# Key scales of the first three pairs and the fold of two halved blocks: one operand moved from SBUF to PSUM

## The chip, the core and the metric

The kernel runs on one core of a Trainium2 chip. A core has five engines that work in parallel, each in program order: TensorE (PE) multiplies matrices into PSUM, VectorE (DVE), ScalarE (ACT) and GpSimd (POOL) work on tiles in SBUF and, DVE and ACT, in PSUM, and SyncE (SP) issues transfers. The engines wait for each other through semaphores. The metric is the device time of one execution in microseconds (us); the time of a version is the median of its runs.

## What is computed

An attention block with a state that is updated token by token (B = 4, H = 8, S = 768, D = 48), and behind it a gated feed-forward layer over 3072 tokens:

```python
k_n = k / (np.linalg.norm(k, axis=-1, keepdims=True) + 1e-06)
state = zeros((B, H, D, D))
for t in range(S):
    y[:, :, t] = einsum('bhd,bhde->bhe', q[:, :, t], state)
    v_old = einsum('bhde,bhd->bhe', state, k_n[:, :, t])
    state += beta[:, :, t] * outer(k_n[:, :, t], v[:, :, t] - v_old)
x = y.transpose(0, 2, 1, 3).reshape(3072, 384)
h = x @ w_in                  # 384 x 2048
out = (h * np.cos(h)) @ w_out # 2048 x 384
```

## The kernel before

**Units and pairs.** The sequence is cut into 24 units of 32 tokens (C = 32). Unit n belongs to pair m = n // 2. Within a unit, the token-by-token recurrence becomes a triangular system: the Gram matrix of the unit's keys (`gram`, line 641, products at L652) goes to PSUM, its strictly triangular part, scaled by the keys' step sizes, is inverted, and the inverse, applied to the values minus what the state gives, yields the state's update. The state passes from unit to unit, so the units form a chain. Beside it the feed-forward layer is spread out over PE, ACT, DVE and POOL as soon as a unit's output rows are there, and the weights are rounded on their way in (`narrow_split` on ACT, L525 and L529; `narrow_shift` on DVE, L533; `narrow_add` on POOL, L537: one per 512 or 384 columns).

**Three kinds of inversion.** Units 0 and 1 are inverted by repeated doubling on PE, with DVE between the steps (`doubling`, lines 681 to 758: L691, L701, L706, products at L736, then L744, L749, L752, L756 on DVE). From unit 4 on, a pair's scaled Gram blocks are written to DRAM (`gram_put`, line 799, DMA issued at L810), read back in another layout (`gram_get`, L823), inverted column by column on POOL (`invert`, L856 and L863, two instructions a column), and returned through DRAM. Pair 1 (`HALVED = 1`, units 2 and 3) goes the same way with halved blocks: each 32 x 32 block is cut into two diagonal blocks of 16 x 16 (HC = 16), put in one tile by `fold` (line 767), and one block between them, which PE applies later from `off_blocks`. Part of pair 1's columns is inverted on DVE.

**Scales.** For the pair's keys, ACT squares (L554), DVE sums (L559), POOL takes the root with a power (`norms_root`, L571) and `scale` on DVE (lines 578 to 595) makes from the norm: `knrm` = norm + 1e-6 (L582), `krec` = 1 / knrm^2 (L584 and L585), `bs` = beta * krec (L587) and `bz`, which is `bs` for one half of the partitions and zero for the other, by a mask `odd` of two columns (L590). Units 0 to 3 have a scale each, of 8 columns; from unit 4 on there is one for a pair, of 16 columns. `weigh` (lines 597 to 612, product at L607) multiplies a pair's values by `knrm`; `gram_keys` (line 660; L664 for units 0 and 1, L673 for the others) multiplies the Gram blocks by `bs` or `bz` on their way from PSUM to SBUF, and `gram_queries` (line 779; L784 or L792) takes the other half of the same bank with a mask.

**The fold before** works on one SBUF tile `g`: it scales its first 16 columns by a mask of the partitions, in place (L770), adds the last 16 columns scaled by the other mask (L771), and writes the last 16 columns by the first mask to `off_blocks` (L775):

```python
f = gs[n] = g[:, :, 0:HC]
nc.vector.tensor_scalar(f, f, in_half[:, 0:1], None, op0=ALU.mult)
nc.vector.scalar_tensor_tensor(
    out=f, in0=g[:, :, HC:], scalar=in_half[:, 1:2], in1=f,
    op0=ALU.mult, op1=ALU.add,
)
nc.vector.tensor_scalar(
    off_blocks[n][:, :, HC:], g[:, :, HC:], in_half[:, 0:1], None, op0=ALU.mult
)
```

**Fillers.** While PE has nothing else to do in the opening, `keep_warm` (lines 490 to 495, product at L492) multiplies a constant tile into `p_out[:, 0]`. `p_out` (line 485) is one PSUM bank of [128, 2, 256] floats; later it takes the feed-forward layer's output products (L1274, L1332). Its columns `[:, 1, 192:]` are used by nothing.

**What sets the order.** The kernel is written as tasks, each with an engine, a cost, what it depends on, and what PSUM bank or SBUF tile it makes or frees (`add(..., deps, makes=..., uses=...)`, from line 1471 on for a unit). Class `Order` (lines 60 to 237) holds the sequence of the tasks as a stored list; `uses` names the buffers whose last use a task is, and a task that makes a buffer can't stand ahead of them. When the tasks are written out, each instruction is pinned behind the one ahead of it on its engine (lines 1862 to 1894), so every engine's order is the stored one, and semaphores for data and buffers come on top. The bank with the tag "two" (one buffer) holds in turn a unit's turned keys and queries (`turn`, L619), its Gram products, and the later products of the state. Transfers that go through SP stand in one queue, and they share eight hardware semaphores in turn, so that a transfer waits for the eighth ahead of it.

Of the kernel before, what the change touches and what calls it, by code (L numbers as in the profile page):

```python
# [13 lines left out]
ALU = mybir.AluOpType  # L14
# [45 lines left out]
class Order:  # L60
# [147 lines left out]
    def add(  # L208
        self, key, engine, cost, emit, deps=(), makes=(), uses=(), moves=0.0, due=1e9,
        other=None,  # L210
    ):
        assert key not in self.tasks, key
        self.tasks[key] = emit, set(deps), makes, uses
        for t in uses:
            self.users[t] = self.users.get(t, 0) + 1
        for tag, t in makes:
            self.tiles[t] = tag
# [22 lines left out]
def kernel(  # L240
# [32 lines left out]
    nc = tc.nc  # L273

    B, H, S, D = q.shape
# [49 lines left out]
    def half(i):  # L325
        return slice(DP * i, DP * i + DP)
# [13 lines left out]
    def by_parity(t):  # L340
        return t.rearrange("p (j a) i -> p a j i", a=2)
# [5 lines left out]
    DOUBLED, HALVED, HC = 2, 1, C // 2  # L347
    eye16 = early[:, EYE : EYE + HC * HC]
    in_flat = in_sum.rearrange("p a b c -> p (a b c)")
    half_zt, off_blocks = (  # L350
        {
            2 + i: t[:, at + i * H * C : at + (i + 1) * H * C].rearrange("p (h c) -> p h c", c=C)
            for i in range(2)
        }
        for t, at in ((early, HALF_ZT), (in_flat, OFFS))
    )
# [75 lines left out]
    odd = consts[:, 128 + C : 130 + C]  # L432
    in_half = consts[:, 130 + C : 132 + C]
# [8 lines left out]
    for b in range(B):  # L442
        nc.gpsimd.dma_start(
            out=bq[C * b : C * b + H].rearrange("p n t -> p (n t)"), in_=beta[b]
# [19 lines left out]
    bt = const.tile([128, NU, H], FP, name="bt")  # L464
# [18 lines left out]

    HM = DM // 2
    p_out = psum.tile([128, 2, 256], FP, name="p_out", tag="o", bufs=1)


    out_begun = []
# [46 lines left out]
    def narrow_add(t):  # L535
# [4 lines left out]
    sums, squares, scales, kq_ts, p_ts, p_gs, gs, grams, gbs, z_drs, zs, zts = (  # L540
        {} for _ in range(12)
    )
# [35 lines left out]
    def scale(m, part):  # L578

        n = part.stop - part.start  # L580
        bs, bz, knrm = (t[:, part] for t in scales[m])
        nc.vector.tensor_tensor(out=knrm, in0=knrm, in1=tiny[:, 0:n], op=ALU.add)  # L582
        krec = work.tile([128, 2, H], FP, name="krec")[:, 0:n]
        nc.vector.tensor_tensor(out=krec, in0=knrm, in1=knrm, op=ALU.mult)  # L584
        nc.vector.reciprocal(krec, krec)  # L585
        first = 2 * m + part.start
        nc.vector.tensor_tensor(  # L587
            out=bs, in0=bt[:, first : first + n], in1=krec, op=ALU.mult
        )
        nc.vector.tensor_tensor(  # L590
            out=bz,
            in0=bs[:, :, :, None].to_broadcast([128, n, H, 2]),
            in1=odd[:, None, None, :].to_broadcast([128, n, H, 2]),
            op=ALU.mult,
        )

    def weigh(m):

        vp, knrm = vps[m], scales[m][2]
        if 2 * m >= PLAIN_TURNS:  # L600

            t = work.tile([128, 2, H], FP, name="krec")
            nc.vector.tensor_copy(t[:, :, 0::2], knrm[:, :, 0::2])
            for i in range(2):
                nc.vector.tensor_copy(t[half(i), :, 1::2], knrm[half(1 - i), :, 1::2])
            knrm = t
        nc.vector.tensor_tensor(  # L607
            out=vp,
            in0=vp,
            in1=knrm[:, :, :, None].to_broadcast([128, 2, H, D]),  # L610
            op=ALU.mult,
        )

    def turn(n, tag):
# [45 lines left out]
    def gram_keys(n):  # L660
        if n < DOUBLED:
            bz = scales[n // 2][1][:, n % 2]
            for par in range(2):
                nc.vector.tensor_tensor(  # L664
                    out=power(n)[:, OFF, par].rearrange("p j (o i) -> p j o i", i=C),
                    in0=p_gs[n][:, par, :, 0, None].to_broadcast([128, NP, 2, C]),
                    in1=bz[:, par::2, :, None].to_broadcast([128, NP, 2, C]),
                    op=ALU.mult,
                )
            return  # L670
        g = gs[n] = work.tile([128, H, C], FP, name="g")
        bs = scales[n // 2][0][:, n % 2]
        nc.vector.tensor_tensor(  # L673
            out=by_parity(g),
            in0=p_gs[n][:, :, :, 0],
            in1=bs.rearrange("p (j a) -> p a j", a=2)[:, :, :, None].to_broadcast(wide),
            op=ALU.mult,
        )


    def power(n):
        whole = (in_sum, w_sum)[n].rearrange("p a b c -> p (a b c)")
        return whole[:, 0 : POWERS * H * C].rearrange(
            "p (x a j i) -> p x a j i", a=2, j=NP, i=2 * C
        )
# [79 lines left out]
        nc.gpsimd.memset(in_flat[:, OFFS : OFFS + 2 * H * C], 0.0)  # L765

    def fold(n):
        g = gs[n]
        f = gs[n] = g[:, :, 0:HC]
        nc.vector.tensor_scalar(f, f, in_half[:, 0:1], None, op0=ALU.mult)  # L770
        nc.vector.scalar_tensor_tensor(  # L771
            out=f, in0=g[:, :, HC:], scalar=in_half[:, 1:2], in1=f,
            op0=ALU.mult, op1=ALU.add,
        )
        nc.vector.tensor_scalar(  # L775
            off_blocks[n][:, :, HC:], g[:, :, HC:], in_half[:, 0:1], None, op0=ALU.mult
        )

    def gram_queries(n):
        if n < DOUBLED:  # L780
# [180 lines left out]
    first, spare = {}, {}  # L961
# [127 lines left out]
    def gate_tile(p, s, unit):  # L1089
        return g_tiles[order.place["gates", p, s, unit]]  # L1090
# [302 lines left out]
    def store(p, i, cols=slice(0, DM)):  # L1393
# [7 lines left out]
        for b in range(B):  # L1401
# [9 lines left out]
            x=2, x_sum=XS, turns=2, g=GATES, o=2, o_out=2,  # L1411
# [3 lines left out]
    add = order.add  # L1415
# [26 lines left out]
    def doubling(n):  # L1442
        add(("double_first", n), "DVE", 0.75, lambda: double_first(n), [("gram_keys", n)])
        add(("double_rest", n), "DVE", 0.7, lambda: double_rest(n), [("double_first", n)],
            uses=[("g_gram", n)])
        last = [[("double_first", n)], [("double_first", n)]]
        for level in range(len(LEVELS)):
            for par in range(2):
                deps = last[par] + ([("double_rest", n)] if level == 1 else [])
                key, tile_of = ("double", n, level, par), ("p_d", n, level, par)  # L1450
                add(key, "PE", 0.6, lambda level=level, par=par: double(n, level, par), deps,
                    makes=[("h", tile_of)])
                last[par] = []
                for what, emit, levels in (
                    ("copy", double_copy, COPIES), ("turn", double_turn, TURNS),
                    ("add", double_add, ADDS),
                ):
                    if level not in levels:
                        continue
                    then = ("double_" + what, n, level, par)  # L1460
                    add(then, "ACT" if what == "copy" else "DVE", 0.35,
                        lambda emit=emit, level=level, par=par: emit(n, level, par),
                        [key], uses=[tile_of])
                    last[par].append(then)
                if level == 3:
                    add(("double_turn", n, 3, par), "DVE", 0.3,
                        lambda par=par: double_turn(n, 3, par), last[par])
                    last[par] = [("double_turn", n, 3, par)]
        return last[0] + last[1]

    def unit(n):
        m, second = n // 2, n % 2
# [17 lines left out]
        part = slice(second, second + 1) if n < 4 else slice(0, 2)  # L1490
# [18 lines left out]
        if n < PLAIN_TURNS:  # L1509
# [6 lines left out]
                uses=[("p_t", n)])  # L1516
        else:
# [11 lines left out]
            uses=[("kq_t", n)])  # L1529
        add(("gram_keys", n), "DVE", 0.46, lambda: gram_keys(n),  # L1530
            [("gram", n), scaled],
            uses=[("p_g", n), ("scales", m)])
        add(("gram_queries", n), "DVE", 0.46, lambda: gram_queries(n), [("gram_keys", n)],
            uses=[("p_g", n)])
        if n < DOUBLED:
            inverted = doubling(n)
        else:
            inverted = [("get", n)]
            if m == HALVED:
                add(("fold", n), "DVE", 0.62, lambda: fold(n), [("gram_keys", n), ("half_tiles",)])  # L1540
            add(("gram_put", n), "SP", 0.45 if n < PLAIN_TURNS else 1.8, lambda: gram_put(n),
                [("fold" if m == HALVED else "gram_keys", n)], makes=[] if second else [("g_dr", ("g_dr", m))],
                uses=[("g_gram", n)], moves=0.85)
            if second:
                inverse(m)
            add(("get", n), "SP", 1.9, lambda: get(n),
                [("put", m)] + ([("clear", i) for i in range(ZTS)] if m != HALVED else []),
                makes=[("zt", ("zt", n))] if m != HALVED else [], uses=[("z_dr", m)], moves=0.9)
# [6 lines left out]
            uses=[("vp", m)] if n else [])  # L1555
        few = 0.7 if n < PLAIN_TURNS else 0.61
        ready = [("right", n)] + inverted
        if m == HALVED:
# [7 lines left out]
                uses=[("p_v", n)])  # L1566
# [3 lines left out]
            uses=[("rhs", n) if n else ("vp", m)] + ([] if n < DOUBLED else  # L1570
                  [("u_half", n)] if m == HALVED else [("zt", n)]))
# [354 lines left out]
```

## Time and profile before

| | us |
|---|---|
| median of 3 runs | 641.02 |
| the three runs | 639.75, 641.02, 642.40 |
| the profiled execution's own time | 643.07 |
| its span in the profile | 641.3 |
| mean granted TensorE clock | 0.989 of full speed |

The profiled execution is a run of its own, above the three timed ones; 1.77 us of it lie outside the span. The profile records when each instruction of each engine began and ended. Its parts used here: the busy time of each engine; the chain of work that ended last, followed back from the end, with for each step its start, its duration, the engine and what it writes and reads; the timeline, which lists instructions in order of time (start, duration of the stretch, engine, line, operation, names and shapes, and in square brackets the idle time ahead of it with what ended it; a row that ends in "x6" is a group of six records of one kind); and the table of windows, which gives for a stretch its length and then, for each engine in turn, the busy time and the number of instructions, in the order PE, PEld (weight loads), DVE, ACT, POOL, and then the granted TensorE clock, the busy share of the DMA engines and their GB/s.

Of the lines that the change touches, the trace has in the first 65 us: L582 five times, with a mean of 0.156 us; L584 0.169, L585 0.213, L587 0.168 and L590 0.187, also five times; L607 0.95 to 1.04 in the four products that read `knrm` itself; L770, L771 and L775 twice each. L607 reads `knrm` through a copy from pair 4 on (0.96 to 1.02). The filler L492 stands 70 times in the records, all between 1.3 and 80.1 us.

### The profile page before, as it was taken

What the parts mean: (1) busy time and instruction counts of PE and PEld (TensorE: products, weight loads), DVE (VectorE), ACT (ScalarE), POOL (GpSimd) and SP (SyncE); (2) the same over time, 40 slices, a digit from 0 to 9 for tenths busy, and PEclk for the clock granted to TensorE, in tenths of its full rate; (3) what the DMA queues carried; (4) which work ended last, traced back from release to release, by engine and by line L of the source; (5) the groups of instructions that cost most, each with busy time, mean ns of one, the idle gap of its engine ahead of it and who ended that gap; (6) DMA issues with size and microseconds to landing.
All of it is one profiled execution on the core that took longest, in us unless ns stands there. A gap on an engine that the chain in (4) does not pass through costs nothing.

```text
span 641.3 us, 24183 instructions
## 1 busy us (share of the span) xinstructions
PE 622.4 (97%) x10174; PEld 578.0 (90%) x10174; DVE 495.7 (77%) x1030; ACT 297.2 (46%) x528; POOL 435.2 (68%) x775
## 2 busy tenths in 40 slices
PE   7997989999999999999999999999999999999997
PEld 5776877987799999999999999999999999999997
DVE  5896556679989998898787898888888776666682
ACT  3655556554234453543543634743643553545440
POOL 4274688588788788887898887886883883112231
PEclk7999899999999999999999999999999999999999
DMA  9886646854435541655416345243304102000001
GB/s 190 215 180 165 145 100 139 169 102 65 95 58 77 94 67 34 113 87 99 76 23 105 51 72 100 52 62 66 74 2 82 41 2 42 18 2 26 2 25 26
DMA packets 209382, 50.37 MB, mean 79 GB/s; under 512 B 200921, under 2 KB 204281, under 8 KB 209273
## 3 DMA queue, kind: packets, MB, share of 16 engines
q1 hardware_dynamic: 159224, 35.62, 29.3%
q10 hardware_dynamic: 49744, 12.66, 9.8%
q8 instruction: 80, 1.31, 0.9%
q0 software_dynamic: 304, 0.54, 0.4%
q14 instruction: 30, 0.24, 0.1%
HBM read 38.55 MB, written 10.22 MB: 76 GB/s over the span
## 4 chain that ended last, share of the span: by engine, by line
PE 77%; DMA 6%; POOL 6%; DVE 5%; issue 2%; SPq 1%; ACT 1%; ACTq 0%; DVEq 0%; POOLq 0%
PE p_out L1332 26%; PE p_h L1250 25%; PE p_h L1076 6%; PE p_kq L907 3%; PE p_s L1004 3%; PE p_out L1274 3%; POOL part L856 2%; POOL z L863 2%; PE p_u L979 2%; PE p_kq L1034 2%; DMA kp<-in_k_dram 2%; PE p_g L652 2%; DMA gb<-g_dr 2%; PE p_h L1332 2%; DMA g_dr<-g 1%
## 5 line engine op out<-in xcount | busy, mean ns | idle before, releaser
L856 POOL TENSOR_TENSOR part<-z,gb 128x126 f32<-128x126 f32 (+24 forms) x317 | 140.2, 442 | 44.6 <-DMA gb<-g_dr 12.4
L863 POOL TENSOR_TENSOR z<-z,part 128x126 f32<-128x126 f32 (+24 forms) x317 | 145.2, 458 | 24.9
L1332 PE MATMUL p_out<-w_out,g_ffn 128*128 128x192 f32 x672 | 122.3, 329 | 0.1
L1332 PEld LDWEIGHTS p_out<-w_out,g_ffn 128*128 128x128 f32 x672 | 107.7, 191 | 1.4 <-DVE o L1384 0.3
L1129 ACT ACTIVATE turns<-turns,halfpi 128x512 f32<-128x512 f32 x96 | 68.3, 719 | 79.9 <-DVE turns L1120 57.1
L1332 PE MATMUL p_out<-w_sum,g_ffn 128*128 128x192 f32 x496 | 88.4, 328 | 0.7 <-DVE o L1384 0.7
L1250 PE MATMUL p_h<-x_sum,w_in 128*128 128x128 f32 x640 | 84.0, 278 | 0.9 <-DVE x_sum L1165 0.6
L1332 PEld LDWEIGHTS p_out<-w_sum,g_ffn 128*128 128x128 f32 x496 | 79.7, 191 | 1.4 <-DVE o L1384 0.7
L1250 PEld LDWEIGHTS p_h<-x_sum,w_in 128*128 128x128 f32 x640 | 78.5, 192 | 2.4 <-ACT o L1371 0.9
L1113 ACT ACTIVATE turns<-g_ffn,quarter_turn 128x512 int32<-128x512 f32 x70 | 50.0, 719 | 55.6 <-DVE g_ffn L1267 28.7
L1120 DVE SCALAR_TENSOR_TENSOR turns<-g_ffn,turns 128x512 f32<-128x512 f32 x70 | 54.9, 786 | 14.7 <-ACT turns L1113 14.5
L1267 DVE TENSOR_TENSOR g_ffn<-g_ffn,p_h 128x512 f32<-128x512 f32 x80 | 54.0, 678 | 12.5 <-PE p_h L1250 11.8
L1047 ACT COPY y<-p_kq 32x384 f32<-32x384 f32 x96 | 45.1, 470 | 37.9 <-PE p_kq L1034 23.3
L1132 DVE TENSOR_TENSOR g_ffn<-turns,g_ffn 128x512 f32<-128x512 f32 x70 | 53.3, 769 | 4.4 <-ACT turns L1129 4.4
L1250 PE MATMUL p_h<-x_sum,in_sum 128*128 128x128 f32 x400 | 53.4, 278 | 0.0
L1250 PEld LDWEIGHTS p_h<-x_sum,in_sum 128*128 128x128 f32 x400 | 49.5, 192 | 1.0
L1384 DVE SCALAR_TENSOR_TENSOR o<-p_out,o 128x192 f32<-128x192 f32 x74 | 25.1, 351 | 29.5 <-PE p_out L1332 29.1
L571 POOL TENSOR_TENSOR knrm<-ksum,halves 128x16 f32<-128x16 f32 (+1 forms) x14 | 36.5, 2609 | 14.7 <-DVE ksum L559 14.7
L1076 PE MATMUL p_h<-x_ffn,w_in 128*128 128x128 f32 x384 | 46.0, 278 | 0.0
L1076 PEld LDWEIGHTS p_h<-x_ffn,w_in 128*128 128x128 f32 x384 | 44.0, 192 | 0.9
L1250 PE MATMUL p_h<-x_ffn,w_in 128*128 128x128 f32 x320 | 42.4, 278 | 0.0
L1348 POOL TENSOR_TENSOR g_ffn<-g_ffn,g_ffn 128x512 f32<-128x512 f32 x18 | 25.9, 1442 | 23.2 <-PE p_out L1332 19.4
(164 smaller groups left out, 1080.8 us busy)
## 6 DMA issues: line engine op xcount, KB each, us to landing
g_ffn<-in_moe_w_in_dram SPq DMA_DIRECT2D x10, 512.0 KB
g_ffn<-in_moe_w_out_dram SPq DMA_DIRECT2D x10, 384.0 KB
vp<-in_v_dram SPq DMA_DIRECT2D x76, 48.0 KB
gb<-g_dr SPq DMA_DIRECT2D x14, 256.0 KB
kp<-in_k_dram SPq DMA_DIRECT2D x128, 24.0 KB
out_dram<-o SPq DMA_DIRECT2D x14, 192.0 KB
g_ffn<-in_moe_w_out_dram ACTq DMA_DIRECT2D x6, 384.0 KB
zt<-z_dr SPq DMA_DIRECT2D x68, 32.0 KB
```

The costliest lines, as they stand in the source:

```text
L571: nc.gpsimd.tensor_tensor(out=scales[m][2][:, part], in0=sums[m, part.start][:, 0:n], in1=halves[:, 0:n], op=ALU.pow,)
L856: eng.tensor_tensor(out=part, in0=z[:, 0:rows, j, None].to_broadcast(shape), in1=a[:, j, None, j + 1 :].to_broadcast(shape), op=ALU.mult,)
L863: eng.tensor_tensor(out=behind, in0=behind, in1=part, op=ALU.subtract)
L1047: nc.scalar.copy(by_parity(y[quarter(b)]), p_kq[quarter(b ^ 1), :, b % 2])
L1076: nc.tensor.matmul(p_h[:, i], w_in[:, t, (4 * k + i) * 128 : (4 * k + i + 1) * 128], xts[p][:, t, unit * 128 : (unit + 1) * 128], start=(i ...
L1113: nc.scalar.activation(turns[p, f], hidden_of(p, f), AF.Identity, bias=quarter_turn, scale=TURN)
L1120: nc.vector.scalar_tensor_tensor(out=r, in0=hidden_of(p, f), scalar=TURN, in1=t, op0=ALU.mult, op1=ALU.subtract,)
L1129: nc.scalar.activation(r, r, AF.Sin, bias=halfpi, scale=2.0 * math.pi)
L1132: nc.vector.tensor_tensor(out=place(p, f), in0=step_of(rests.pop((p, f)), f), in1=step_of(hidden_of(p, f), f), op=ALU.mult,)
L1250: nc.tensor.matmul(p_h[:, e], in_block(*w)[:, e], x_of(p, b), start=new and e == 0, stop=True, skip_group_check=True,)
L1267: nc.vector.tensor_tensor(out=part_of(p, to), in0=part_of(p, one), in1=part_of(p, two), op=op)
L1332: nc.tensor.matmul(p_o, left(p, part, a)[:, e % 4], right(e, b), start=(e == 0), stop=(e == FT // 2 - 1), skip_group_check=True,)
```

## The change

For the first three pairs (`m < 3`), `scale` keeps its scratch in the unused columns of `p_out` (`spare_out`), in slices of 16 columns. The root's `knrm` stays as POOL wrote it; knrm + 1e-6 goes to the scratch, and (knrm + 1e-6) times it makes the square. `bz` is made from `krec` and beta in two instructions, one for each column of the mask, where one from `bs` stood. `weigh` adds 1e-6 itself for these pairs (0.0 for the others) and so becomes an instruction with a scalar for all twelve pairs. For units 2 and 3, `gram_keys` writes the scaled keys back into their own PSUM bank, and `fold` reads them from there, in four instructions in place of three (the addition is made once for each parity of the heads). Since the fold is now a last user of that bank, it is named in `uses`. The stored order of the tasks is the same, and so is the sequence of instructions on PE, ACT, POOL and SP; DVE has five instructions more for `bz` and two more for the folds.

```diff
     p_out = psum.tile([128, 2, 256], FP, name="p_out", tag="o", bufs=1)
+    BY_PSUM, spare_out = 3, p_out[:, 1, HM:]
...
         bs, bz, knrm = (t[:, part] for t in scales[m])
+        first = 2 * m + part.start
+        beta_here = bt[:, first : first + n]
+        if m < BY_PSUM:
+
+            at = first % 4 * 2 * H
+            krec = spare_out[:, at : at + n * H].rearrange("p (u h) -> p u h", h=H)
+            nc.vector.tensor_scalar(krec, knrm, 1e-6, None, op0=ALU.add)
+            nc.vector.scalar_tensor_tensor(
+                out=krec, in0=knrm, scalar=1e-6, in1=krec, op0=ALU.add, op1=ALU.mult
+            )
+            nc.vector.reciprocal(krec, krec)
+            nc.vector.tensor_tensor(out=bs, in0=beta_here, in1=krec, op=ALU.mult)
+            for x in range(2):
+                nc.vector.scalar_tensor_tensor(
+                    out=bz[:, :, :, x], in0=krec, scalar=odd[:, x : x + 1], in1=beta_here,
+                    op0=ALU.mult, op1=ALU.mult,
+                )
+            return
...
-        nc.vector.tensor_tensor(
+        nc.vector.scalar_tensor_tensor(
             out=vp,
-            in0=vp,
-            in1=knrm[:, :, :, None].to_broadcast([128, 2, H, D]),
-            op=ALU.mult,
+            in0=knrm[:, :, :, None].to_broadcast([128, 2, H, D]),
+            scalar=1e-6 if m < BY_PSUM else 0.0,
+            in1=vp,
+            op0=ALU.add,
+            op1=ALU.mult,
         )
...
         bs = scales[n // 2][0][:, n % 2]
+        keys = by_parity(g)
+        if n // 2 == HALVED:
+
+            keys = folded[n] = p_gs[n][:, :, :, 0]
         nc.vector.tensor_tensor(
-            out=by_parity(g),
+            out=keys,
             in0=p_gs[n][:, :, :, 0],
...
     def fold(n):
-        g = gs[n]
-        f = gs[n] = g[:, :, 0:HC]
-        nc.vector.tensor_scalar(f, f, in_half[:, 0:1], None, op0=ALU.mult)
-        nc.vector.scalar_tensor_tensor(
-            out=f, in0=g[:, :, HC:], scalar=in_half[:, 1:2], in1=f,
-            op0=ALU.mult, op1=ALU.add,
-        )
+        g, f = folded.pop(n), gs[n][:, :, 0:HC]
+        gs[n] = f
+        f = by_parity(f)
+        nc.vector.tensor_scalar(f, g[:, :, :, 0:HC], in_half[:, 0:1], None, op0=ALU.mult)
+        for par in range(2):
+            nc.vector.scalar_tensor_tensor(
+                out=f[:, par], in0=g[:, par, :, HC:], scalar=in_half[:, 1:2], in1=f[:, par],
+                op0=ALU.mult, op1=ALU.add,
+            )
         nc.vector.tensor_scalar(
-            off_blocks[n][:, :, HC:], g[:, :, HC:], in_half[:, 0:1], None, op0=ALU.mult
-        )
+            by_parity(off_blocks[n][:, :, HC:]), g[:, :, :, HC:], in_half[:, 0:1], None,
+            op0=ALU.mult,
+        )
...
-                add(("fold", n), "DVE", 0.62, lambda: fold(n), [("gram_keys", n), ("half_tiles",)])
+                add(("fold", n), "DVE", 0.62, lambda: fold(n), [("gram_keys", n), ("half_tiles",)],
+                    uses=[("p_g", n)])
```

More of the change, by code (lines that the diff above doesn't have):

```diff
@@ L767, in fold @@
     def fold(n):
-        g = gs[n]
-        f = gs[n] = g[:, :, 0:HC]
-        nc.vector.tensor_scalar(f, f, in_half[:, 0:1], None, op0=ALU.mult)
-        nc.vector.scalar_tensor_tensor(
-            out=f, in0=g[:, :, HC:], scalar=in_half[:, 1:2], in1=f,
-            op0=ALU.mult, op1=ALU.add,
-        )
-        nc.vector.tensor_scalar(
-            off_blocks[n][:, :, HC:], g[:, :, HC:], in_half[:, 0:1], None, op0=ALU.mult
-        )
+        g, f = folded.pop(n), gs[n][:, :, 0:HC]
[7 more added lines that the diff above has]
+            )
+        nc.vector.tensor_scalar(
+            by_parity(off_blocks[n][:, :, HC:]), g[:, :, :, HC:], in_half[:, 0:1], None,
+            op0=ALU.mult,
+        )
+    folded = {}
     def gram_queries(n):
```

## The prediction

> **What bounds the kernel now.** I read the page's engine shares first, then the chain of waits, then the timelines of PE, DVE and POOL over the first 65 us, where every touched instruction stands (the twelve weighing products, L607, run on to 522 us).
>
> ```profile
> PE 622.4 (97%) x10174; PEld 578.0 (90%) x10174; DVE 495.7 (77%) x1030; ACT 297.2 (46%) x528; POOL 435.2 (68%) x775
> ```
>
> PE is the bound. Its idle stretches of over 0.3 us sum to about 11 us before 90 us, and hardly any follow. From there PE works without a pause in a fixed order, so what the opening gains or loses arrives at the end unchanged. The opening is bound by a chain that crosses the engines:
>
> ```profile
> 41.42 4.54 DMA g_dr<-g
> ...
> 46.04 5.13 DMA gb<-g_dr
> ...
> 54.91 5.80 DMA kp<-in_k_dram
> ```
>
> Unit 3's folded block is written out at 41.42 and read back; behind that, SP issues the loads of keys that land at 60.70, and PE waits for what follows. The put's start is set by DVE:
>
> ```profile
> 35.70 1.03 DVE L607 TENSOR_TENSOR vp<-vp,knrm 128x768 f32<-128x768 f32 x1
> 36.65 1.31 DVE L770 TENSOR_SCALAR g<-g,consts 128x128 f32<-128x128 f32 x1
> 38.00 1.28 DVE L771 SCALAR_TENSOR_TENSOR g<-g,consts 128x128 f32<-128x128 f32 x1
> ...
> 39.40 0.41 DVE L673 TENSOR_TENSOR g<-p_g,bs 128x256 f32<-128x256 f32 x1
> ...
> 40.73 0.27 DVE L770 TENSOR_SCALAR g<-g,consts 128x128 f32<-128x128 f32 x1
> 41.04 0.35 DVE L771 SCALAR_TENSOR_TENSOR g<-g,consts 128x128 f32<-128x128 f32 x1
> ```
>
> The same two fold instructions take 1.31 and 1.28 us for unit 2, and 0.27 and 0.35 us for unit 3. POOL tells why:
>
> ```profile
> 34.43 1.48 POOL L537 TENSOR_TENSOR w_in<-w_in,g_ffn 128x512 uint32<-128x512 uint32 x1
> ...
> 35.87 2.01 POOL L537 TENSOR_TENSOR w_in<-w_in,g_ffn 128x512 uint32<-128x512 uint32 x1
> ...
> 37.84 1.30 POOL L537 TENSOR_TENSOR w_in<-w_in,g_ffn 128x512 uint32<-128x512 uint32 x1
> ```
>
> L770 ends 0.08 us after one POOL addition (37.88), L771 0.15 us after the next (39.13). The 35.87 addition took 2.01 instead of 1.30 because L607 ran ahead of it. [...]
>
> **What the change removes.** With the keys in PSUM, the fold has one SBUF tensor at most. Rows that read PSUM beside POOL are not stretched (L673 is 0.41 at all 22 places, by its line's own view), so unit 2's stall goes: (1.31 - 0.27) + (1.28 - 0.35) = 1.97 us.
>
> **What it adds.**
> 1. *Fold.* L771 becomes two instructions of 64 elements. L924 (PSUM, pointer scalar, 192 elements) takes 0.41: 0.20 of elements and 0.21 fixed; so 0.27 each, and they overlap: +0.1 per fold.
> 2. *Scales.* Six instructions take the place of five: bz is written by two, 0.21 each, overlapped: +0.15 to 0.18 for each of four scales before the fold. L607 stays at two SBUF inputs, so no gain there; the small scale instructions show 0.17 each in the rows, so no stall is left to remove in them.
> 3. *Writing PSUM from DVE.* No row shows it. Reading costs nothing extra (L664, 256 elements, 0.414: 0.147 fixed; L691, SBUF, 512 elements, 0.681: 0.148). The dearest surcharge in the rows is that of a pointer scalar (L924 0.407 against L1384 0.354 at the same size, 0.053). Bounds: 0 and 0.053 on 24 scale instructions, 0 to 1.3 us; nothing in a write can make it cheaper than the SBUF row. I take 0, the nearest row. [...]
> 4. *Waits on p_out.* The order of all engines is unchanged, but the scratch lies in p_out's bank, which PE's fillers (L492) write. The built program has waits in both directions: each scale's first instruction waits for the last filler issued ahead of it, and the next filler waits for the scale's last instruction; PE is in order, so all matmuls behind that filler wait too.
>
> ```profile
> 11.12 1.22 PE L492 MATMUL p_out<-o 128*128 128x256 f32 x2
> ...
> 27.09 1.56 PE L492 MATMUL p_out<-o 128*128 128x256 f32 x6
> 28.59 1.09 PE L736 MATMUL p_h<-in_sum 64*64 64x128 f32 x16
> 29.61 0.70 PE L492 MATMUL p_out<-o 128*128 128x256 f32 x2
> ...
> 37.05 0.86 PE L652 MATMUL p_g<-kq_t 48*32 48x64 f32 x64
> ```
>
> ```profile
> 11.37 0.17 DVE L582 TENSOR_TENSOR knrm<-knrm,tiny 128x8 f32<-128x8 f32 x1 [0.61 <-POOL knrm L571]
> ...
> 27.55 0.16 DVE L582 TENSOR_TENSOR knrm<-knrm,tiny 128x8 f32<-128x8 f32 x1
> ...
> 29.18 0.12 DVE L582 TENSOR_TENSOR knrm<-knrm,tiny 128x8 f32<-128x8 f32 x1
> 32.27 0.45 DVE L752 STREAM_TRANSPOSE w_sum<-p_h 128x256 f32<-128x256 f32 x1 [1.10 <-PE p_h L736]
> ```
>
> The shifts against before, in order:
> - First scale: from 11.37 to the filler's end, 12.34: +1.0, with bz +1.18. POOL's next root (13.78, then L582 at 15.83) waits for DVE, so this goes on. The filler of the second scale ends at 15.75 and does not bind; bz makes +1.36.
> - Third scale: DVE is ready at 27.55 + 1.36 = 28.91. The fillers of 27.09 start at 28.45; it waits for the second of their three calls, 1.13 later: 29.6, +2.06, with bz +2.24.
> - The third call now waits for that scale (30.8) where PE was free at 29.6. Then the L736 group (1.09, some of it overlapped) and the filler follow, to 33.04. The fourth scale, due at 29.18 + 2.24 = 31.42, waits for it: 33.08, +3.90, with bz +4.08.
> - The next filler waits for that scale, but DVE's old idle 1.10 before 32.27 takes up 0.87: +3.21 at L673.
> - The queries (L792) now wait for the keys' write instead of overlapping it: +3.32 at L607.
> - Fold 2 without its stall ends at 40.96, +1.47 against 39.48.
> - Unit 3's Gram products (37.05) go into the bank that fold 2 still reads: before they waited for the queries alone, now for the fold's end. They start at 40.96 and the keys at 41.85: +2.45. So 0.98 of the 1.85 gained is given back.
> - Unit 3's put: +2.60. Its landing, POOL and DVE's inversion, and the key loads behind it on SP follow it; PE's own later lag (+3.6) meets its idle 1.38 before 55.96.
>
> 5. *L607 against POOL.* POOL's additions are released by DVE's shifts (L533), +3.21; L607 is at +3.32. Before, L607 started 0.17 ahead of the 35.87 addition; now 0.06 ahead (39.01 against 39.07). Behind, it would wait until about 0.13 before that addition's end (as L607 got started 0.13 before 35.90) and lose 1.16, all of it before fold 2. I take it as lost: any extra time in writing the keys to PSUM uses up 0.06.
>
> **Sum**: 2.60 + 1.16 = +3.76, say +3.7. The profiled execution took 643.07 (span 641.3 and 1.77 around it), above the three timed runs (639.75 to 642.40), so it would become 646.8; on the median of 641.02 the forecast is **644.7 us**.
>
> [...]
>
> **Rivals.**
> - *L607 slips through.* All as above without the 1.16: 643.6. For it: the margin is still positive. 26%.
> - *PSUM writes cost.* 1.3 on top: 646.0. 12%.
> - *Another stretch at half clock.* The granted clock was 0.50 for 6.8 us after PE's idle at 60 to 63.5:
>
> ```profile
> 60.00:63.50 3.50, 1.35 (x36) 1.07 (x32) 1.82 (x4) 2.69 (x6) 1.08 (x3) 1.00 0.31 114
> 63.50:70.30 6.80, 6.62 (x86) 5.66 (x88) 3.75 (x10) 3.28 (x7) 5.62 (x4) 0.50 0.74 131
> ```
>
>   The groups in it (L979 2.06 against 1.08 elsewhere, L492 2.08 against 1.13, L1004 1.56 against 0.89, L1022 2.14 against 1.49) cost 3.25. PE's new idle near 30 us (1.2 in 3.4) could bring a second: 648. 6%.
> - *Faster.* The same place decides. PE was busy 39% of 60 to 63.5 and lost the clock; at 53.3 to 56.7 it idled 1.38 of 3.4 (60% busy) and kept it. If the waits on p_out were covered, the fold alone would bring keys 3 and the put about 0.7 earlier (37.05 becomes 37.75 for the Gram products, and 39.40 becomes 38.65), the idle would shrink by that, to near 60% busy, and the 3.25 would go too: 641.0 - 0.7 - 3.3 = 637.0. It takes effect once the put stands 0.5 us earlier; against it are the four scales above. 8%.
> - *Nothing to see*: filler and scale happen to miss each other and the gain is given back at the Gram products: 641. 6%.
>
> **Numbers.** Forecast 42%. About 0.5%, or 3.2 us, is what a measurement here tells from no change: 637.8 to 644.2. The first wait depends on when the clock was low (at full clock that filler takes 0.60 and costs next to nothing), so each slower case has some 1 us either way: the forecast lies above 644.2 in seven of ten, the first rival in two. Slower 0.42 x 0.7 + 0.26 x 0.2 + 0.12 + 0.06 = 0.52; faster 0.08; within 0.40. The range, 641.0 to 647.0, leaves out the faster case, the clock case and the tails.
>
> **What would show it.** Right: the first scale starting at a filler's end; a PE gap ended by DVE ahead of a filler near 30 us; fold instructions all near 0.3; a POOL addition between L607's queueing and its run; the put of unit 3 some 2.6 to 3.8 later. Wrong: scales at their old times, or the put before 41.42. The first scale and the fourth are the two largest terms.

## The result: 0.2 to 0.4% slower

In the comparison that belongs to the change, the changed kernel took 641.59 us (median of 22 runs) and the kernel before, run beside it, 639.55: a ratio of 1.0043, 95% interval [1.0028, 1.0059], or 2.0 us by the medians and 2.8 by the ratio (0.0043 x 641). Two further sets of runs (below) gave 1.0016 [0.9992, 1.0040] and 1.0037 [1.0010, 1.0065]. The mean of all is 642.04 over 46 runs against 639.91 over 92: 2.1 us. The forecast was 3.7 us, with a range of 641.0 to 647.0. So the sign and the mechanism of the loss in the opening were right, the size was too large by one term, and the way from the opening to the end was another than forecast.

**The profile after** (own time 644.44, span 642.6, clock 0.995). Its engine shares:

```profile
PE 619.7 (96%) x10174; PEld 575.5 (90%) x10174; DVE 494.6 (77%) x1037; ACT 297.1 (46%) x528; POOL 437.4 (68%) x775
```

PE has 2.7 us less of busy time than before (622.4), though it does the same work: the stretch at half clock near 64 us is missing. The waits on p_out stand where the forecast put them. DVE's timeline, with the starts of the first, third and fourth scale (L589) and the idle time ahead of each:

```profile
12.73 0.17 DVE L589 TENSOR_SCALAR p_out<-knrm 128x8 f32<-128x8 f32 x1 [1.69 <-PE p_out L493]
...
29.78 0.17 DVE L589 TENSOR_SCALAR p_out<-knrm 128x8 f32<-128x8 f32 x1 [0.70 <-PE p_out L493]
...
33.37 0.17 DVE L589 TENSOR_SCALAR p_out<-knrm 128x8 f32<-128x8 f32 x1 [1.81 <-issue]
```

The third has PE's filler (L493) as its releaser; at the fourth the profile names none, but the start follows a filler's end by 0.10 us (33.27, next fence). PE's timeline shows the other direction:

```profile
28.54 1.13 PE L493 MATMUL p_out<-o 128*128 128x256 f32 x4
30.92 0.70 PE L493 MATMUL p_out<-o 128*128 128x256 f32 x2 [1.25 <-DVE bz L596]
31.55 1.09 PE L761 MATMUL p_h<-in_sum 64*64 64x128 f32 x16
32.57 0.70 PE L493 MATMUL p_out<-o 128*128 128x256 f32 x2
...
34.51 0.70 PE L493 MATMUL p_out<-o 128*128 128x256 f32 x2 [0.37 <-DVE bz L596]
...
41.52 0.85 PE L673 MATMUL p_g<-kq_t 48*32 48x64 f32 x64 [0.80 <-DVE in_sum L802]
```

Two of the three filler calls of a group run at 28.54; the third waits 1.25 us for the scale's last instruction. L673 at 41.52 is unit 3's Gram products, which wait for fold 2's last instruction. DVE around that fold:

```profile
39.43 0.92 DVE L626 SCALAR_TENSOR_TENSOR vp<-knrm,vp 128x768 f32<-128x768 f32 x1
40.27 0.34 DVE L796 TENSOR_SCALAR g<-p_g,consts 128x128 f32<-128x128 f32 x1
40.64 0.48 DVE L798 SCALAR_TENSOR_TENSOR g<-p_g,consts,g 128x64 f32<-128x64 f32 x2
41.03 0.34 DVE L802 TENSOR_SCALAR in_sum<-p_g,consts 128x128 f32<-128x128 f32 x1
42.41 0.43 DVE L698 TENSOR_TENSOR p_g<-p_g,bs 128x256 f32<-128x256 f32 x1 [1.03 <-PE p_g L673]
```

The stall of 1.31 and 1.28 us is gone, and DVE then stands idle for 1.03 us ahead of unit 3's keys (L698).

**Where the time went and came back.** The start of four things on PE, and its last end, in the executions profiled (us):

| | before | before, again | after | after, 2nd | after, 3rd |
|---|---|---|---|---|---|
| unit 3's Gram products | 37.05 | 39.52 | 41.52 | 41.27 | 41.07 |
| unit 1's state products | 52.80 | 55.27 | 60.84 | 58.40 | 58.47 |
| unit 4's Gram products | 59.20 | 61.52 | 65.67 | 63.23 | 63.31 |
| unit 5's Gram products | 71.08 | 71.73 | 72.56 | 70.12 | 70.20 |
| last end of PE | 637.0 | 635.7 | 638.3 | 635.7 | 634.6 |

From unit 5's Gram products to the end all take 564.0 to 565.9 us, so what stands there arrives at the end, but only to within 1.9 us, which is coarse beside a loss of 2.1. Between units 4 and 5 the changed kernel needs 6.89 us three times, the kernel before 11.88 and 10.21. Windows of the trace of after, at the two stretches that the prediction shows for before:

```profile
60.00:63.50 3.50, 3.50 (x98) 3.26 (x97) 3.12 (x14) 1.96 (x4) 0.38 (x2) 1.00 0.83 232
63.50:70.30 6.80, 6.50 (x153) 5.52 (x151) 5.75 (x19) 6.80 (x15) 5.86 (x14) 1.00 0.39 88
```

PE is busy nearly throughout (3.50 of 3.50 and 6.50 of 6.80 us) and keeps the full clock, where before it was busy 1.35 of 3.50 us and then ran 6.8 us at 0.50. PE comes so late that what it had waited for is there.

### The profile page after: what moved, and what is told of

The parts are those of the page before. It is cut to its first block, busy times and chain, and to the rows that moved or that the text cites. A ratio compares the mean times of both kernels' runs of the same rounds, so it can differ in the third digit from the quotient of the medians.

```text
span 642.6 us, 24195 instructions
## 1 busy us (share of the span) xinstructions
PE 619.7 (96%) x10174; PEld 575.5 (90%) x10174; DVE 494.6 (77%) x1037; ACT 297.1 (46%) x528; POOL 437.4 (68%) x775
## 3 DMA queue, kind: packets, MB, share of 16 engines
q8 instruction: 80, 1.31, 0.9%
## 4 chain that ended last, share of the span: by engine, by line
PE 82%; POOL 5%; DVE 4%; issue 3%; DMA 3%; SPq 1%; ACT 1%; ACTq 0%; DVEq 0%; POOLq 0%
PE p_out L1362 27%; PE p_h L1280 25%; PE p_h L1106 7%; PE p_kq L937 3%; PE p_out L1304 3%; PE p_s L1034 3%; PE p_kq L1064 2%; POOL z L893 2%; POOL part L886 2%; PE p_g L673 2%; PE p_u L1009 2%; PE p_h L1362 2%; PE p_h L761 2%; PE p_out L493 1%; PE p_z L1085 1%
## 5 line engine op out<-in xcount | busy, mean ns | idle before, releaser
L886 POOL TENSOR_TENSOR part<-z,gb 128x126 f32<-128x126 f32 (+24 forms) x317 | 145.0, 457 | 46.3 <-DMA gb<-g_dr 12.2
L893 POOL TENSOR_TENSOR z<-z,part 128x126 f32<-128x126 f32 (+24 forms) x317 | 141.4, 446 | 24.8
```

What stands on the lines that cost most here:

```text
L886: eng.tensor_tensor(out=part, in0=z[:, 0:rows, j, None].to_broadcast(shape), in1=a[:, j, None, j + 1 :].to_broadcast(shape), op=ALU.mult,)
L893: eng.tensor_tensor(out=behind, in0=behind, in1=part, op=ALU.subtract)
```

## The experiments

All ratios are against the kernel before, run on the same chip beside them. Each kernel here has 12 runs, and the kernel before 35 in each of the three sets (e1 to e4, e5 to e8, e9 to e12).

| kernel | median | ratio and 95% interval |
|---|---|---|
| fold alone (e1) | 640.61 | 0.9996 [0.9970, 1.0021] |
| scales alone (e2) | 643.70 | 1.0035 [1.0010, 1.0060] |
| changed, scratch in SBUF (e3) | 640.35 | 0.9986 [0.9962, 1.0010] |
| before, krec in p_out's corner (e4) | 642.86 | 1.0030 [1.0009, 1.0050] |
| before, three fillers more (e5) | 639.67 | 0.9980 [0.9961, 1.0000] |
| changed, again (e6) | 641.77 | 1.0016 [0.9992, 1.0040] |
| e3 with unit 2's Gram in the other bank (e7) | 639.54 | 0.9983 [0.9959, 1.0006] |
| changed, one weight load later (e8) | 643.25 | 1.0035 [1.0011, 1.0059] |
| before, again (e9) | 639.15 | 0.9995 [0.9971, 1.0019] |
| changed, a third time (e10) | 641.92 | 1.0037 [1.0010, 1.0065] |
| e2 with three fillers more (e11) | 640.82 | 1.0030 [1.0004, 1.0056] |
| e7 with three fillers more (e12) | 639.33 | 0.9994 [0.9969, 1.0018] |

### The two halves of the change (e1, e2)

```diff
-    BY_PSUM, spare_out = 3, p_out[:, 1, HM:]
+    BY_PSUM, spare_out = 0, p_out[:, 1, HM:]
```

> Only the fold reads PSUM; the scales are those of before. Theory (the loss is the scales' waits on p_out; the fold's stall goes, and part of it is given back because unit 3's Gram products wait for fold 2): L770 and L771 of unit 2 near 0.35 us in place of 1.31 and 1.28, unit 3's put 0.4 to 1.0 us before its 41.42, no idle of PE ahead of a filler, and a time of 0 to 1 us under before, or 3 to 4 us under it if the half-clock stretch near 63.5 us goes too. Rival (the fold part is what costs: the bank held to the fold's end, seven longer rows): the put at 41.4 or later and 1 to 3 us over before.

The fold without the scales costs nothing and brings nothing that can be told: 0.9996. Its local gain is there (DVE's timeline, unit 2):

```profile
37.91 0.34 DVE L796 TENSOR_SCALAR g<-p_g,consts 128x128 f32<-128x128 f32 x1
38.28 0.48 DVE L798 SCALAR_TENSOR_TENSOR g<-p_g,consts,g 128x64 f32<-128x64 f32 x2
38.67 0.34 DVE L802 TENSOR_SCALAR in_sum<-p_g,consts 128x128 f32<-128x128 f32 x1
```

The put came at 42.38, not before 41.42, but unit 2's keys came late too (35.91 against 34.67): in this execution PE idled 1.06 us ahead of unit 2's queries at 25.46. From keys to put it is 6.47 us, against 6.75 before: 0.28 gained. So the put missed its forecast, but it was late with the keys and not through the fold. The rival's 1 to 3 us over is out but for its lower end, as the interval reaches 1.3 us over. The "3 to 4 us under" missed too: the one profile has no half-clock stretch near 63.5 us, and the time is that of before.

For e2, keys and fold are those of before (`gram_keys` writes to `g`, `fold` has its three instructions and no `uses`), and the scales stay as changed.

> Only the scales use the corner of p_out (and the weighing adds 1e-6); keys and fold are those of before, in SBUF. Theory: the four scales stand where they stand in the changed kernel (+1.1, +1.1, +2.0, +3.9 us), the fold stalls again beside POOL (about 2 us), unit 3's Gram products no longer wait for the fold, unit 3's put is 3.3 to 5 us late, and the time is 2 to 4 us over before. Rival (the fold part is what costs): at most 1 us over before.

The loss is here: 1.0035. The fourth scale waits 1.81 us, and the fold stalls beside POOL again; DVE's timeline:

```profile
32.22 0.17 DVE L589 TENSOR_SCALAR p_out<-knrm 128x8 f32<-128x8 f32 x1 [1.81 <-issue]
...
39.09 1.32 DVE L792 TENSOR_SCALAR g<-g,consts 128x128 f32<-128x128 f32 x1
40.44 1.27 DVE L793 SCALAR_TENSOR_TENSOR g<-g,consts 128x128 f32<-128x128 f32 x1
```

A miss: the put was 2.43 us late (43.85), not 3.3 to 5. The first scale lost only 0.21 us (11.58 against 11.37), since the half clock of the opening set in at 11.45 in this execution and not at 8.91, so that the first filler ended sooner.

### The waits or the instructions (e3, e4)

```diff
-            krec = spare_out[:, at : at + n * H].rearrange("p (u h) -> p u h", h=H)
+            krec = work.tile([128, 2, H], FP, name="krec")[:, 0:n]
```

> The changed kernel with one line altered: the scales' scratch is an SBUF tile, all instructions and the fold as changed. Theory: without p_out there is nothing to wait for; the scales stand at their old times but for bz's second instruction (0.15 to 0.18 each, 0.6 in all at unit 2's keys), unit 3's put is within 0.5 us of 41.42, and the time is within 1.5 us of before, 2 to 3 us under the changed kernel. Rival (the longer forms and the fold's bank cost, not the waits): still 2 to 3 us over before.

With the same instructions and the same fold, and only the scratch elsewhere, the time is that of before: 0.9986. The first scale starts at 11.29, right behind POOL's root, and PE's fillers run without a break. PE's timeline:

```profile
28.04 1.56 PE L493 MATMUL p_out<-o 128*128 128x256 f32 x6
...
38.87 0.85 PE L672 MATMUL p_g<-kq_t 48*32 48x64 f32 x64 [0.79 <-DVE in_sum L801]
```

The wait at unit 3's Gram products stays, as it belongs to the fold. The put came 0.88 us late, more than the 0.5 expected; 0.70 of it stands already at the second scale.

```diff
         krec = work.tile([128, 2, H], FP, name="krec")[:, 0:n]
+        if m < 3:
+            at = (2 * m + part.start) % 4 * 2 * H
+            krec = spare_out[:, at : at + n * H].rearrange("p (u h) -> p u h", h=H)
```

> The kernel before with one tile moved: krec of the first three pairs lies in the corner of p_out; five instructions of the old forms, the old weighing, the old fold. Theory: the waits on p_out alone give most of the loss: the third scale near 29.5 us, the fourth near 32.5, PE idle ahead of a filler near 30 us, unit 2's keys 2.2 to 2.8 us late, the time 1.5 to 4 us over before. Rival (the waits are covered, and the new forms cost): the time of before within 1 us.

The old five instructions with one tile in p_out's corner lose 0.30%, as much as the new scales. DVE waits ahead of the instruction that first writes there (L588), and PE behind it (last line, from PE's timeline):

```profile
12.45 0.18 DVE L588 TENSOR_TENSOR p_out<-knrm 128x8 f32<-128x8 f32 x1 [0.84 <-PE p_out L493]
...
29.17 0.17 DVE L588 TENSOR_TENSOR p_out<-knrm 128x8 f32<-128x8 f32 x1 [0.55 <-PE p_out L493]
...
32.23 0.18 DVE L588 TENSOR_TENSOR p_out<-knrm 128x8 f32<-128x8 f32 x1 [1.50 <-PE p_out L493]
...
29.84 0.70 PE L493 MATMUL p_out<-o 128*128 128x256 f32 x2 [0.71 <-DVE bs L591]
```

Here the profile names the filler at the fourth scale too. Together the two runs show that the place of the scratch makes the loss, and not the forms of the instructions or the fold.

### The rest of the fold's gain (e7)

```diff
-        add(("gram", n), "PE", 0.64, lambda: gram(n, tag),
+        add(("gram", n), "PE", 0.64, lambda: gram(n, "kq" if n == 2 else tag),
```

with the same tag in `makes`, and the task ("state", 0), which issues nothing, moved to stand behind the fold, so that the bank is free.

> The kernel with the scratch in SBUF, and unit 2's Gram products in the other bank (kq), so that unit 3's no longer wait for fold 2; every engine's order is the same. Theory (0.8 to 1.0 us of the fold's gain was given back there): no wait of PE for L801, unit 3's Gram products right behind the fillers, unit 3's put 0.5 to 1.0 us earlier against unit 2's keys than in the kernel with the scratch in SBUF (there 6.68 us after them), and a time 0 to 1 us below that kernel's. Rival (the bank does not bind, something else holds unit 3): put and time as in that kernel.

Unit 3's Gram products no longer wait; PE's timeline:

```profile
37.57 1.13 PE L493 MATMUL p_out<-o 128*128 128x256 f32 x4
38.63 0.86 PE L672 MATMUL p_g<-kq_t 48*32 48x64 f32 x64
```

From keys to put it is 5.57 us, 1.11 less than in e3: the bank did hold back that part. The time is 0.9983 against 0.9986, which the intervals don't tell apart.

### The clock near 64 us (e5, e9, e11, e12)

```diff
+        if (n, level, par) == (1, 5, 1):
+            keep_warm()
+            keep_warm()
```

in `double`, and one more call for n == 1 in `solve`, in all three kernels with fillers.

> The kernel before with three more fillers on PE, two ahead of the last products of unit 1's doubling and one ahead of its solve, in the idle time between 60 and 63.7 us, where the profile of before shows PE 39% busy and then 6.8 us at half the clock. Theory (PE's idle there brings the half-clock stretch, and that costs about 3 us in the executions that have it): granted clock 1.00 from 60 to 74 us, PE at unit 2's Gram products (71.08) some 2.5 to 3.3 us earlier, the time 1 to 3 us under before. Rival (the clock has nothing to do with that idle time): clock 0.50 again, the time of before or up to 0.5 us over it.

> The kernel before as it is, for a second profiled execution and to see how far apart two sets of runs of one kernel come out. Theory (every kernel with the fold in SBUF has PE idle for half of the 3.4 us near 61 us and then a half-clock stretch; none with the fold in PSUM has): half clock for 3.4 or 6.8 us between 60 and 74 us, ratio 1.000 within 0.002. Rival (the stretch in the first profile was chance): full clock there, the span 2 to 3 us under 641.3.

> The kernel with the scales alone changed, and three more fillers in the idle time near 61 us (two ahead of the last products of unit 1's doubling, one ahead of its solve). Theory (the half-clock stretch hangs on PE's idle there and costs 1.5 to 3 us; the waits cost 3.2 us whatever the clock): no stretch or half of one, and 0.5 to 2.5 us over before, where the kernel without the fillers was 2.2 over. Rival (the fillers only take PE's time): as without them or above.

> Scratch in SBUF, fold from PSUM, unit 2's Gram products in the other bank, and the three fillers near 61 us: what the runs so far point to as the fastest. Theory: no waits on p_out, no fold stall, none of the wait at unit 3's Gram products, full clock to 74 us; 637.5 to 640 us, 1.5 to 3.5 us under before. Rival (the put is not what sets the end, and that kernel had no half-clock stretch to lose): the time of the kernel without the fillers, 1 us under before, or the fillers' own 0.5 us over that.

The four profiles with the fold in SBUF and no more fillers (before twice, e2, e4) all had the stretch, 3.41 or 6.83 us long; those with the fold in PSUM (after three times, e1, e3, e7, e8, e12) had none there. (Most of these kernels have a single profile.) In e5 the fillers did not remove it but it was 3.41 us, in e11 it was gone. What e5's fillers could not fill was idle time of another kind: PE stood 1.77 us up to 60.97, ahead of the first of them (61.45), with no releaser but "issue" (see the next section). Its unit 5's Gram products (the 71.08 that the expectation calls unit 2's) start at 69.77, 1.3 us earlier and not 2.5 to 3.3. Windows of e9, of e5 and of e12, each the 3.41 us ahead of a half-clock stretch and the first 3.41 us of it:

```profile
63.85:67.26 3.41, 2.29 (x50) 1.95 (x51) 2.90 (x8) 3.41 (x8) 2.58 (x1) 1.00 0.46 68
67.26:70.67 3.41, 3.41 (x46) 2.66 (x46) 2.34 (x5) 1.51 (x4) 2.66 (x4) 0.50 0.76 117
```

```profile
58.46:61.87 3.41, 1.64 (x49) 1.31 (x41) 0.00 (x0) 0.79 (x2) 1.43 (x6) 1.00 0.65 236
61.87:65.28 3.41, 3.41 (x22) 1.91 (x20) 2.89 (x7) 2.80 (x7) 2.30 (x1) 0.50 0.41 66
```

```profile
23.00:26.41 3.41, 1.62 (x16) 1.14 (x11) 2.19 (x7) 0.92 (x3) 1.26 (x1) 1.00 0.89 210
26.41:29.82 3.41, 3.41 (x24) 2.76 (x24) 0.72 (x3) 2.18 (x4) 0.00 (x0) 0.50 0.73 193
```

Each follows a window in which PE idled, and e12's lies at 26 us, where PE waited 1.79 us ahead of a unit's turned queries. In the time, little of it is seen: the fillers brought 0.20% [0.00, 0.39] in before (where the mean granted clock of the 12 runs rose to 0.9959, from 0.9927 in the 35 beside them), and no difference that can be told in e2 (1.0030 against 1.0035) or e7 (0.9994 against 0.9983). e12, meant as the fastest, is not shown to beat the kernel before; nor is e3 or e7, whose intervals hold 1.

### PE's idle time without a name (e6, e8, e10)

In the profile of after PE stood idle twice where the waits name only "issue":

```profile
PE p_kq L1052 <- issue: 1.7, 1, 1.7
PE p_out L493 <- DVE bz L596: 1.6, 2, 1.3
PE p_h L761 <- issue: 1.5, 1, 1.5
```

They end at 48.32, inside a group of equal products, and at 56.22. The trace has transfers of 16,384 bytes in the queue of kind "instruction"; one landed at 46.67 and one at 54.76, 1.65 and 1.46 us ahead of those ends. For the first I blamed a weight load that stands ahead of it, and moved the load by its place in the stored order (task 2120 from behind 107 to ahead of 2095).

> The changed kernel with one weight load of 512 KB moved behind unit 3's put and the next keys in SP's queue; nothing else. Theory (PE's gap of 1.49 us at 46.83 is a block of PE's instructions that comes late, because its fetch stands behind that load in the DMA engines): the instruction packet comes at 42.5 to 44 us in place of 45.74 and the gap at 47 us is gone; PE's lag is 1.5 us smaller near 50 us, of which 0 to 1.5 us reach the time. Rival (the gap has another cause): the gap stays, the time is that of the changed kernel.

> The changed kernel once more, for a second profiled execution. Theory (what its profile shows after 44 us belongs to the kernel, not to that one execution): PE idles again about 1.5 us in the middle of a group of products near 47 us and 1.7 us near 55 us with nothing that the profile names, is 7 to 8 us late against before near 60 us, waits little from 60 to 64 us and keeps the full clock to 74 us; time 1.5 to 4 us over before. Rival (chance of one execution): the gaps stand elsewhere or are missing, and the half clock comes in as in before.

> The changed kernel a third time, beside the kernel before on the same chip. Theory: the scales' waits as in both earlier profiles (PE idle 1.26 and 0.37 us ahead of two fillers near 30 and 34 us), full clock from 20 to 74 us, the nameless gaps near 47 and 55 us of another size again, 1 to 3.5 us over before. Rival (waits are made good later): the time of before within 0.5 us.

The idle time near 47 us was missing in e8, but in e6 and e10 as well, with the load in its old place: e8 tells nothing of the load. The one ahead of L1052 came back in both, shorter, and in e8 another of 1.04 us stood at 40.99. From PE's waits in e10:

```profile
PE p_kq L1052 <- issue: 1.4, 1, 1.4
```

The waits on p_out are the same to 0.01 us in all three profiles (1.26 and 0.37 us); the nameless idle time between 44 and 57 us is 3.1, 0.8 and 1.4 us. My theory that both gaps belong to the kernel fell: their place and size belong to the execution. The ends of such idle time in after, e6, e8 and e10, and of the one inside unit 6's Gram products in before (89.51), stand 1.3 to 1.7 us behind the landing of an instruction block; in e5 it is 1.77 us (59.20 to 60.97). Such blocks land 4 to 12 us apart in the first 100 us (3.9 to 9.7 in before, 3.8 to 12.4 in after). That PE waited for them is argued from this, not shown. What would make a block late was not settled.

## Why the prediction was nearly right, and where it was not

- **Waits on p_out** (item 4): right, step by step. The profiled execution began 0.28 us later than before (the first norm's sum at 9.30, not 9.03), to be taken off each number. First scale +1.0 forecast, +1.08 measured; third +2.06 and +1.95; fourth +3.90 and +3.91; unit 2's keys +3.21 and +3.32. In the second and third profile the first wait was shorter, 1.27 and 1.43 us against 1.69 (in the second the mean granted clock of the first 20 us was 0.91, against 0.83): within the 1 us either way that the prediction left for it.
- **Fold** (what it removes, item 1): right in the main. From L607's start to fold 2's end it was 3.77 us and is 1.94, a gain of 1.83 where 1.85 was forecast. The longer form costs more than the 0.1 taken: unit 3's fold takes 1.11 us (43.75 to 44.86) against 0.86. Its two scalings of 128 elements take 0.34 us each from PSUM (L796, L802) where they took 0.27 and 0.28 from SBUF, so "Reading costs nothing extra" (item 3), which was read from TENSOR_TENSOR rows, does not hold for them; why is not shown. Unit 3's put is 2.92 us late, forecast 2.60; keys to put gained 0.40, forecast 0.61.
- **Writing PSUM** (item 3): 0 was the right end. L589 and L590 take 0.17 us, as L582 and L584 did; the reciprocal 0.22 in place of 0.20; the keys 0.42 in place of 0.41. None of these four is shorter than its SBUF row.
- **L607 against POOL** (item 5): the step that failed. I took its 0.06 us of margin as lost, 1.16 us, a term that no run shows. (The 0.13 us in its working is 0.21 by the timeline, 35.70 against 34.43 + 1.48 = 35.91; the term hardly changes.) DVE kept it: L626 starts at 39.43, the addition that it had to precede at 39.46, as POOL's timeline shows:

```profile
39.46 2.03 POOL L538 TENSOR_TENSOR w_in<-w_in,g_ffn 128x512 uint32<-128x512 uint32 x1
```

  The addition took 2.03 us, as when DVE ran ahead of it before (2.01). The margin was 0.03 to 0.04 us in all three profiles, so the first rival ("L607 slips through", 26%) is what happened. Without that term the sum is 2.60, and the runs show 2.0 to 2.8; that the two agree is in part luck, as the next point shows.
- **From the put to the end** (item 4's last point and "Sum"): wrong in mechanism, though not much in size. I let the put set the end and PE's lag be taken up by 1.38 us of idle time. In all three profiles of after PE itself was the later: 5.6 to 8.0 us behind the first profile of before at unit 1's state products (3.1 to 5.6 behind the second), with 0.8 to 3.1 of it nameless idle time, and no wait for the key loads between 56.3 and 74 us. It took up idle time of 1.38, 1.30 and 1.03 us, and the half-clock stretch did not come. So the "Faster" rival had the right place and price for the clock, but the stretch goes because PE is late, not because the put is early.
- **Half clock a second time** (6%): did not happen in the changed kernel, though it had windows of 3.41 us with 1.92 us (from 46.33) and 1.75 us (from 53.16) of PE's busy time.

**Open.** In the profiled executions the loss is not there at the end: their own times are 643.07 and 641.76 for before, and 644.44, 641.75 and 640.96 for after, where the timed runs say +2.1 us. That most timed executions of before keep the full clock near 64 us does not explain it. Their mean granted clock is on record: 63 of 117 lie at 0.992 or below, as the two profiled ones do (0.989 and 0.992), against 7 of the 46 of after. The mean does not say where in an execution the half clock lay. Among the executions at 0.994 or above the changed kernel is still the slower: 641.50 against 639.99 in the set of e6, 641.15 against 638.28 in that of e10. What is left is that five profiled executions are few: both of before lie above the mean of the timed runs (639.91), and single executions of before go from 636.0 to 647.3. How the waits in the opening become 2 us at the end is not shown by any profile.

## What to carry to other kernels

A scratch in an unused corner of a PSUM bank that another engine writes was not free here (1.0030 in e4): fillers and scratch share no column of p_out, and yet the waits ran in both directions, in the changed kernel up to 1.69 us of DVE for a filler and 1.25 us of PE for a scale, and what stood behind them on PE came later too. Look for a bank that only the engines of that step touch, or stay in SBUF (0.9986 in e3). Moving one operand to PSUM did remove a stall of DVE beside POOL (1.31 us became 0.34, and 1.28 became 0.48), but the bank was then held longer, and the next user of the bank gave a good part of it back (1.11 us, by e7 against e3); count that user in. In an opening full of idle time, ask which of the late chains is the later at the first point where all meet, and not only how late the changed one is.

## What the runs showed of the hardware that was not expected

- **The granted clock** halved for 3.41 or 6.83 us after windows of 3.41 us in which PE was busy 1.22 (e2), 1.24 (before), 1.62 (e12), 1.64 (e5) and 1.67 us (e4), and stayed full after 1.75 and 1.92 us in after. The windows ahead of the half-clock stretches of the opening, 0.89 to 1.58 us (1.37 in before, 1.43 in after), fit with this. That would put the border at about half a window (49 to 51%), inside the 39% to 60% that the prediction had; but e9's halved after a window with 2.29 us, so it is no rule. PE was busy for over a third of each of the six windows outside the opening (1.22 of 3.41 us at the least), so such a window was not an idle one.
- **One execution is not the other, near 26 us.** Ahead of unit 2's queries PE idled 0 us in before, but 1.06 (e1), 0.68 (e7), 1.39 (e9) and 1.79 us (e12), put down by the profile to a load of queries or keys; in e1, e7 and e12 an instruction block landed 1.2 to 1.8 us ahead too, so that these may be the other kind. The changed kernel, 1.45 us later at that point, did not idle there in any of its three profiles, so that a part of its loss would be covered in such executions; this was not tested.
